# Threshold attention with a two-layer MLP: PV moved to the end of a period, third tile's weights on another engine at the start, last copy split by rows

## The chip, the cores and the metric

The kernel runs on one core of one Trainium2 chip. The metric is the time of one execution on the device in microseconds (us), as the median of several runs; lower is better. The profile of one execution shows five engines, which run side by side and wait for each other through semaphores: TensorE (PE, with its weight loads as PEld), VectorE (DVE), ScalarE (ACT), GpSimd (POOL) and SyncE (SP, which issues most of the DMA transfers).

## The reference

There are 8 batches of 8 heads with 576 tokens of 64 values. Per head, scores are formed, those further than tau below the row's maximum are dropped, the rest go through a softmax, and the result is multiplied by V. The heads of a token, side by side, give a row of 512 values, and two dense layers with a leaky ReLU between them follow.

```python
def _attn_ref(q, k, v, tau):
    scale = 1.0 / np.sqrt(q.shape[-1])
    scores = scale * np.matmul(q, k.transpose(0, 1, 3, 2))
    thresh = np.max(scores, axis=-1, keepdims=True) - tau
    scores = np.where(scores >= thresh, scores, -1000000000.0)
    scores = scores - np.max(scores, axis=-1, keepdims=True)
    attn = np.exp(scores)
    attn = attn / (np.sum(attn, axis=-1, keepdims=True) + 1e-09)
    return np.matmul(attn, v)            # (8, 8, 576, 64)

x = attn_out.transpose(0, 2, 1, 3).reshape(4608, 512)
h = x @ moe_w_in                         # (512, 2048)
out = np.maximum(0.01 * h, h) @ moe_w_out  # (2048, 512)
```

## The kernel before

**Periods.** The attention is cut into 72 periods, n = 0 to 71. A period is one block of 128 query tokens (index m) for four heads (two pairs, index pp), or a "tail": the last 64 tokens of all heads of a batch. Two periods with the same tokens give the 128 x 512 input x of one group of the dense layers, so there are 36 groups. The order of instructions on every engine is the order in which the program issues them; there is no scheduler that reorders. The loop over n issues the work of one period, and the work of three different periods is in it: the scores of period n, the transposing of the weights of period n - 1 (`before`), and the product with V of period n - 2 (`due`, `PV_LAG = 2`).

**What a period does, in TensorE's order.** `scores` (L296) writes four tiles of 128 x 576 scores into five PSUM banks `sc`; each is the sum of three products of half-precision parts. `turn` (L186) transposes q and k of a batch to come, 16 transposes in most periods. `spread` (L401) turns the reciprocal row sums of `due`. Then come two halves. Each has up to two `layer2` steps (L470, 128 x 512 into the bank `o`) and one `layer1` unit (L457, a quarter of a group's hidden layer). The first half also has `pv(due)` (L417, 20 matmuls) behind its layer 1 and, in periods 0 to 2, 5, 7 and 8, four 32-bit transposes `turn32(late)` (L211) ahead of PV.

**VectorE.** `copy_min` (L332) copies each score tile to SBUF with its sign changed and takes the row minimum. `recip` (L376) and the thresholds (L347) follow. Then `evacuate(due)` (L436, L428 for tails) scales the PV product into x, and `weights` (L369) applies the mask to three tiles. In periods with `late`, `take_low` (L239) stands between the first and the second mask.

**ScalarE.** It copies the turned parts of q and k (L249), the spread reciprocals (L407), computes the exponentials `exp_plain` (L358) of the three tiles that VectorE masks, the leaky ReLU of layer 1 (L460), and all of the fourth tile's weights: `exp_steep` does a steep Prelu (L363) and an exponential that sums the row (L364). Every second period it copies a finished output block out of `o` (L478). `take_high` (L232) is its part of the 32-bit transposes.

**Transposed weights.** From period 3 on the weights `w` of a period are transposed by a DMA that SP issues in the following period (`turn_w`, L380). For periods 0 to 2 TensorE does it (`turn_w_here`, L388) and `take_w` (L393) copies the result on ScalarE and VectorE; the steps for tiles 2 and 3 are at the start of the next period. GpSimd splits q and k into two halves (L160, L167, L171); the first such step of a period waits for the last mask of the period before.

**Layer queues.** `evacuate` puts four layer-1 units on the list `l1q` when a group's x is complete. `layer1` takes one, and puts the two layer-2 steps that follow from it on `pending`; `settle` moves `pending` to `l2q`, and is called at the start of every `layer1`. So a layer-2 step runs two halves after its unit.

**Buffers.** The results of `turn`, `turn32`, `spread`, `layer1` and `pv` share two PSUM buffers with the tag "h". In the scores of periods 0 to 2 a no-op on ScalarE (L325), from period 3 on one on GpSimd, signals between two row halves that share a bank.

**The end.** The last group's output is copied by ScalarE (L475, columns 0 to 255) and VectorE (L476, columns 256 to 511), and stored by two DMAs, one on ScalarE's queue and one on SP's (L492).

Of the kernel before, what the change touches and what calls it, by code (L numbers as in the profile page):

```python
# [33 lines left out]
def kernel(  # L34
# [10 lines left out]
    nc = tc.nc  # L45
# [309 lines left out]
    def exp_plain(st, n):  # L355
        t = TILES[n]
        st.e[t] = sb.tile([128, 576], FP16, tag=f"e{n}", bufs=1, name="e")
        nc.scalar.activation(out=st.e[t][:, :], in_=st.s[t][:, :], func=AF.Exp, bias=st.mn[:, n : n + 1], scale=-1.0)  # L358

    def exp_steep(st, n):  # L360
        c, h = t = TILES[n]
        z = st.s[t][:, :]
        nc.scalar.activation(out=z, in_=z, func=AF.Prelu, bias=st.th[:, n : n + 1], scale=-1.0, alpha=1e20)  # L363
        nc.scalar.activation(out=w_of(st, t), in_=z, func=AF.Exp, bias=minus_tau[:, :], scale=1.0,  # L364
                             accum_out=st.sum[:, c, h : h + 1])
# [26 lines left out]
    def take_w(st, first, n, o, copy):  # L392
        return copy(out=st.wt[:, :, :, :].rearrange("k c n q -> k (c n) q")[:, ds(first, n), :],  # L393
                    in_=o.rearrange("k (n q) -> k n q", q=128))
# [14 lines left out]
    def pv(st):  # L409
        st.pv = ps.tile([128, 2, 128], FP32, tag="h", bufs=2, name="pv")  # L410
        n = 64 if st.tail else 128
        for c, u in ((c, u) for c in range(2) for u in range(128 // n)):
            pair = 2 * c + u if st.tail else 2 * st.pp + c
            for i in range(5):
                for h in range(2):
                    blk = i if h == 0 else 9 - i
                    nc.tensor.matmul(out=st.pv[ds(64 * h, 64), c, ts(u, n)], lhsT=v16[st.b % 2][:, pair, blk, :],  # L417
                                     rhs=st.wt[:, c, blk - (blk > 4), ts(u, n)],
                                     start=(i == 0), stop=(i == 4), skip_group_check=True)
# [44 lines left out]
    def layer2():  # L464
        g, r = l2q.pop(0)
        if r == 0:
            g.o = ps.tile([128, 512], FP32, tag="o", bufs=1, name="o")
        for j in (2 * r, 2 * r + 1):
            for c in range(2):
                nc.tensor.matmul(out=g.o[ds(64 * c, 64), :], lhsT=g.g[:, j, ds(64 * c, 64)],  # L470
                                 rhs=w_out16[:, j, :], start=(j == 0), stop=(j == 15), skip_group_check=True)
        if r == 7:
            g.out = sb.tile([128, 512], FP32, tag="osb", bufs=3, name="osb")
            if g.where == (B - 1, 3):
                nc.scalar.activation(out=g.out[:, 0:256], in_=g.o[:, 0:256], func=AF.Copy, bias=0.0, scale=1.0)  # L475
                nc.vector.tensor_copy(out=g.out[:, 256:512], in_=g.o[:, 256:512])  # L476
            else:
                nc.scalar.activation(out=g.out[:, :], in_=g.o[:, :], func=AF.Copy, bias=0.0, scale=1.0)  # L478
            stores.append(g)

    def store():
        g = stores.pop(0)
        b, m = g.where
        if m is None:
            for u in range(2):
                nc.sync.dma_start(out=out[ds((b + u) * S + MAIN, 64), :], in_=g.out[ds(64 * u, 64), :])
        else:
            rows = out[ds(b * S, MAIN), :].rearrange("(p t) f -> p t f", t=4)
            parts = (nc.scalar, nc.sync) if g.where == (B - 1, 3) else (nc.sync,)
            for i, eng in enumerate(parts):  # L490
                f = ts(i, 512 // len(parts))
                eng.dma_start(out=rows[:, m, f], in_=g.out[:, f])  # L492


    loads_at, turns_at, early32, late32, split_at_, pool_at = {}, {}, {}, {}, {}, {}
# [120 lines left out]
    while n < N + PV_LAG or l1q or pending or l2q or stores:  # L616
        st = periods[n] if n < N else None
        before = periods[n - 1] if 1 <= n <= N else None
        due = periods[n - PV_LAG] if PV_LAG <= n < N + PV_LAG else None
        here = before and before.n < 3  # L620
        keys, now32, late = turns_at.get(n, []), early32.get(n, []), late32.get(n)


        if st:
            scores(st)
        bank = turn(keys) if keys else None
        for x in now32:
            turn32(x)
        if here:
            before.wt = sb.tile([128, 2, 9, 128], FP16, tag="wT", bufs=4, name="wT")  # L630
            bank = ps.tile([128, 1024], FP16, tag="h", bufs=2, name="tp")
        if due:
            bank = spread(due, bank)
        if here:
            turn_w_here(before, 12, 6, bank[:, 0:768])
        for key in keys:
            take(key, 0, on_act)
        if due:
            take_spread(due, bank)
        for x in now32:  # L640
            take_high(x)
        if here:
            take_w(before, 12, 6, bank[:, 0:768], on_act)
        if st:
            copies(st, before, lambda: [take(key, 1, on_dve) for key in keys], now32)
            exp_plain(st, 0)
        elif before:
            recip(before)
        work = [lambda key=key: split_pool(key) for key in split_at_.get(n, [])] + pool_at.get(n, [])
        for i, f in enumerate(work):  # L650
            mm = f()
            if i == 0 and before:
                behind_masks(mm, before)
        for key in keys:
            if key[1:] == ("t", "k"):
                widen_keys(key[0])
        if n < 4:
            idle((16, 10, 8, 4)[n], spare("o"))
        if here:
            o = ps.tile([128, 1024], FP16, tag="o", bufs=1, name="wp")  # L660
            if n < 3:
                turn_w_here(before, 0, 8, o)
        elif before and st:
            turn_w(before)
        landed = [f() for f in loads_at.get(n, [])]
        while stores:
            store()
        if n == 0:

            for i in range(4):  # L670
                tc.add_manual_dep(load_w(i).ins, w_behind.ins.name, BEHIND, reason="DMA would serve w_in first")


        if due and (n == 3 or n > N):
            pv(due)
            if n > N:
                evacuate(due)
        if n == 3:
            turn_w_here(before, 0, 8, o)
            idle(12, spare("h"))  # L680
        for half in range(2):
            if half == 1 and n == 3:
                exp_steep(st, 3)
            for _ in range(2):
                if l2q:
                    layer2()
            if l1q:
                layer1()
            elif n >= N:
                settle()  # L690
            if half == 0:
                if st:
                    exp_plain(st, 1)
                    exp_plain(st, 2)
                if here:
                    take_w(before, 0, 8, o, on_act)
                if late:
                    turn32(late)
                    take_high(late)
                if n == N:  # L700

                    before.wt = sb.tile([128, 2, 9, 128], FP16, tag="wT", bufs=4, name="wT")
                    free = [(sc[:, ts(i, 512)].bitcast(FP16), 8 * i, m) for i, m in enumerate((8, 8, 2))]
                    for o, first, m in free:
                        turn_w_here(before, first, m, o)
                if due and n <= N:
                    if n != 3:
                        pv(due)
                    evacuate(due)
                if n == N:  # L710
                    a, *more = [take_w(before, first, m, o[:, 0 : 128 * m], on_dve if first else on_act)
                                for o, first, m in free]
                    for x in more:
                        tc.declare_no_dep(x.ins, a.ins, reason="other banks")
            elif st and n != 3:
                exp_steep(st, 3)
        if here:
            o = ps.tile([128, 512], FP16, tag="o", bufs=1, name="wp")
            turn_w_here(before, 8, 4, o)
        for i in range(3 if st else 0):  # L720
            weights(st, i)
            if late and i == 0:
                take_low(late)
            if here and i == 1:
                take_w(before, 8, 4, o, on_dve)
        n += 1
# [1 line left out]
_INS = ['q', 'k', 'v', 'tau', 'moe_w_in', 'moe_w_out']  # L728
# [31 lines left out]
```

## Time and profile before

| | |
|---|---|
| median of 3 runs | 483.85 us (482.97 to 485.55) |
| the profiled execution | 484.76 us; its span, from the first to the last instruction, is 482.9 us |
| granted TensorE clock | 1.00 in all of the span |
| busy: PE, DVE, ACT, POOL | 465.4, 434.8, 418.4, 190.9 us |
| chain that ended last | PE 75%, DMA 13% (12% of it the transposed weights), ACT 6% |
| one mask (L369), one score copy (L332) | 0.816 us, 0.753 us |
| one plain exponential (L358) | 0.778 us |
| steep pair (L363, L364) | 0.767 and 0.775 us, and 0.187 us for reading the sum |
| x from PV (L436) | 0.424 us |

"Busy" is the time in which an engine works on an instruction; the share of the span is that over 482.9 us. The times of one instruction are means of start to end, and successive instructions of an engine overlap a little, so that a mask takes 0.74 us from start to start. The chain is followed back from the last instruction, at each step to what released it. The starts of the score products mark the periods in the trace: period 5 begins at 43.13 us, period 9 at 71.69, period 71 at 455.95.

### The profile page before, as it was taken

How to read it: one execution, taken by the hardware profiler on the slowest of the kernel's cores; microseconds unless marked ns; L12 is line 12 of the kernel's file. 1: busy time of each engine (PE TensorE's matmuls, PEld its weight loads, DVE VectorE, ACT ScalarE, POOL GpSimd, SP SyncE). 2: the span in 40 equal slices, each digit the busy share in tenths (PEclk: the TensorE clock that was granted, in tenths of full speed). 3: DMA queues.
4: the chain of work that ended last, by engine and by line, in shares of the span. 5: the costliest groups of instructions: out<-in, count | busy, mean ns of one | idle time of the engine just before them, and what ended most of it. 6: DMA issues, size and time to landing. Idle time of an engine off the chain costs nothing.

```text
span 482.9 us, 25246 instructions
## 1 busy us (share of the span) xinstructions
PE 465.4 (96%) x10858; PEld 378.9 (78%) x10858; DVE 434.8 (90%) x1315; ACT 418.4 (87%) x777; POOL 190.9 (40%) x313
## 2 busy tenths in 40 slices
PE   7779999999999999999999999999999999999996
PEld 5567788888887788888887788888878888777785
DVE  4999989999999999999999999999998999999940
ACT  3888889999998899998998999999998899988862
POOL 2544436543554444353454554353454444000000
PEclk9999999999999999999999999999999999999999
DMA  9999998898979989799989969898989988657851
GB/s 177 237 210 218 193 224 167 160 192 194 190 165 207 182 165 188 151 177 192 193 167 215 209 142 189 150 194 181 203 167 184 215 168 135 124 122 123 122 96 45
DMA packets 216480, 83.68 MB, mean 173 GB/s; under 512 B 186032, under 2 KB 211888, under 8 KB 216368
## 3 DMA queue, kind: packets, MB, share of 16 engines
q1 hardware_dynamic: 210672, 77.42, 83.2%
q0 software_dynamic: 4224, 4.19, 5.3%
q8 instruction: 85, 1.39, 1.2%
q10 hardware_dynamic: 1472, 0.46, 0.4%
q14 instruction: 27, 0.22, 0.1%
HBM read 36.70 MB, written 9.44 MB: 96 GB/s over the span
## 4 chain that ended last, share of the span: by engine, by line
PE 75%; DMA 13%; ACT 6%; DVE 2%; issue 2%; SPq 0%; POOL 0%; ACTq 0%; POOLq 0%; DVEq 0%
PE hp L457 22%; PE o L470 22%; PE sc L296 18%; DMA wT<-w 12%; PE pv L417 8%; PE tp L401 3%; PE tp L186 2%; ACT e L358 1%; DVE w L369 1%; ACT w L364 1%; DMA vrawt<-in_v_dram 1%; ACT s L363 1%; ACT wT L393 1%; DMA raw<-in_k_dram 1%; DVE s L332 1%
## 5 line engine op out<-in xcount | busy, mean ns | idle before, releaser
L332 DVE TENSOR_SCALAR_CACHE_REDUCE s<-sc 128x576 f32<-128x576 f32 x288 | 205.4, 753 | 15.9 <-PE sc L296 15.8
L457 PEld LDWEIGHTS <-win 128*64 128x64 f16 x4608 | 146.8, 110 | 29.1 <-issue 1.4
L369 DVE SCALAR_TENSOR_TENSOR w<-s,th,e 128x576 f16<-128x576 f32 x216 | 166.3, 816 | 0.2
L358 ACT ACTIVATE e<-s,mn 128x576 f16<-128x576 f32 x216 | 159.7, 778 | 0.0
L470 PE MATMUL o<-wout,g 128*64 128x512 f16 x1152 | 149.3, 379 | 0.5 <-issue 0.5
L457 PE MATMUL hp<-x,win 128*64 128x128 f16 x4096 | 136.7, 219 | 0.3 <-DVE kT L249 0.3
L460 ACT ACTIVATE g<-hp 128x512 f16<-128x512 f32 x144 | 86.2, 598 | 44.5 <-PE hp L457 44.5
L296 PE MATMUL sc<-kT,qT 64*128 64x384 f16 (+7 forms) x1920 | 119.6, 284 | 0.7 <-DVE kT L239 0.7
L296 PEld LDWEIGHTS <-qT 64*128 64x128 f16 (+1 forms) x1920 | 90.3, 97 | 16.4 <-issue 1.4
L160 POOL TENSOR_SCALAR scaled<-raw 128x512 f32<-128x512 f32 x53 | 32.8, 620 | 169.0 <-DVE w L369 158.5
L470 PEld LDWEIGHTS <-g 128*64 128x64 f16 x1152 | 58.9, 110 | 28.6 <-ACT g L460 0.3
L171 POOL TENSOR_TENSOR half<-scaled,half 128x512 f16<-128x512 f32 (+1 forms) x68 | 71.8, 1056 | 5.8
L417 PE MATMUL pv<-wT,v 128*64 128x128 f16 (+1 forms) x1600 | 53.3, 215 | 4.9 <-DMA wT<-w 3.7
L364 ACT ACTIVATE w<-s,minus_tau 128x576 f16<-128x576 f32 x72 | 55.8, 775 | 2.3
L363 ACT ACTIVATE s<-s,th 128x576 f32<-128x576 f32 x72 | 55.2, 767 | 0.0
L417 PEld LDWEIGHTS <-v 128*64 128x64 f16 x1600 | 45.8, 110 | 6.6 <-PE hp L457 4.5
L167 POOL CAST half<-scaled 128x512 f16<-128x512 f32 (+1 forms) x68 | 38.4, 564 | 4.4
L436 DVE TENSOR_TENSOR x<-pv,by 128x256 f16<-128x256 f32 x64 | 27.1, 424 | 9.4 <-PE pv L417 5.7
L407 ACT COPY by<-tp 128x256 f16<-128x256 f16 x72 | 26.8, 372 | 3.4 <-PE tp L388 3.4
L186 PEld LDWEIGHTS <-half 64*128 64x128 f16 x968 | 24.4, 95 | 2.4 <-issue 1.5
L186 PE MATMUL tp<-ident,half 64*128 64x64 f16 x968 | 24.4, 190 | 0.0
L113 POOL CAST v<-vraw 128x256 f16<-128x256 f32 x64 | 24.1, 410 | 0.0
(58 smaller groups left out, 311.9 us busy)
## 6 DMA issues: line engine op xcount, KB each, us to landing
vraw<-in_v_dram SPq DMA_DIRECT2D x16, 512.0 KB, 5.2
out_dram<-osb SPq DMA_DIRECT2D x31, 256.0 KB, 5.0
raw<-in_q_dram SPq DMA_DIRECT2D x13, 512.0 KB, 5.6
raw<-in_k_dram SPq DMA_DIRECT2D x13, 512.0 KB, 4.9
win<-in_moe_w_in_dram POOLq DMA_DIRECT2D x4, 512.0 KB, 11.2
wout<-in_moe_w_out_dram POOLq DMA_DIRECT2D x4, 512.0 KB, 14.9
raw<-in_q_dram SPq DMA_DIRECT2D x12, 128.0 KB, 3.9
raw<-in_k_dram SPq DMA_DIRECT2D x10, 128.0 KB, 4.2
```

The source lines that it names most:

```text
L171: nc.gpsimd.tensor_tensor(out=halves[key][:, 1, 0:n, :, :], in0=scaled.pop(key)[:, 0:n, :, :], in1=halves[key][:, 0, 0:n, :, :], op=AX.sub ...
L186: nc.tensor.transpose(tps[key][r][:, x, t, :], half[rows, x, t, :, :].rearrange("p h d -> p (h d)"), ident[rows, rows])
L296: yield nc.tensor.matmul(out=o, lhsT=lhs, rhs=turned[st.b, "k"][rows, kx, pair, ds(key0, n)], start=(i == 0), stop=(i == 2), skip_group_ch ...
L332: return nc.vector.tensor_scalar(out=st.s[TILES[n]][:, :], in0=sc[:, ds(PLACE[TILES[n]], 576)], scalar1=-1.0 / UNIT, scalar2=None, op0=AX. ...
L358: nc.scalar.activation(out=st.e[t][:, :], in_=st.s[t][:, :], func=AF.Exp, bias=st.mn[:, n : n + 1], scale=-1.0)
L363: nc.scalar.activation(out=z, in_=z, func=AF.Prelu, bias=st.th[:, n : n + 1], scale=-1.0, alpha=1e20)
L364: nc.scalar.activation(out=w_of(st, t), in_=z, func=AF.Exp, bias=minus_tau[:, :], scale=1.0, accum_out=st.sum[:, c, h : h + 1])
L369: st.last = nc.vector.scalar_tensor_tensor(out=w_of(st, t), in0=st.s[t][:, :], scalar=st.th[:, n : n + 1], in1=st.e[t][:, :], op0=AX.is_le ...
L417: nc.tensor.matmul(out=st.pv[ds(64 * h, 64), c, ts(u, n)], lhsT=v16[st.b % 2][:, pair, blk, :], rhs=st.wt[:, c, blk - (blk > 4), ts(u, n)] ...
L457: nc.tensor.matmul(out=hp[ds(64 * c, 64), jj, :], lhsT=w_in16[:, i, ds(128 * (4 * u + jj) + 64 * c, 64)], rhs=g.x[:, i, :], start=(i == 0) ...
L460: nc.scalar.activation(out=g.g[:, ds(4 * u, 4), :], in_=hp[:, :, :], func=AF.Prelu, bias=0.0, scale=1.0, alpha=0.01)
L470: nc.tensor.matmul(out=g.o[ds(64 * c, 64), :], lhsT=g.g[:, j, ds(64 * c, 64)], rhs=w_out16[:, j, :], start=(j == 0), stop=(j == 15), skip_ ...
```

## The change

From period 5 to period 71 `pv(due)` is issued behind both halves, as TensorE's last product of a period, and `evacuate(due)` behind the three masks. Periods 2 to 4 and 72 on keep their order. A half without a layer-1 unit now calls `settle` in every period, not only from period 72 on. In periods 1 and 2 the third tile's weights are computed by `exp_steep` on ScalarE, in the second half, instead of by `exp_plain` and a mask on VectorE. The last output block is copied by rows instead of columns: ScalarE takes rows 0 to 63, VectorE rows 64 to 127, declared independent of each other, and the two stores are split the same way.

```diff
@@ layer2
             if g.where == (B - 1, 3):
-                nc.scalar.activation(out=g.out[:, 0:256], in_=g.o[:, 0:256], func=AF.Copy, bias=0.0, scale=1.0)
-                nc.vector.tensor_copy(out=g.out[:, 256:512], in_=g.o[:, 256:512])
+                a = nc.scalar.activation(out=g.out[0:64, :], in_=g.o[0:64, :], func=AF.Copy, bias=0.0, scale=1.0)
+                x = nc.vector.tensor_copy(out=g.out[64:128, :], in_=g.o[64:128, :])
+                tc.declare_no_dep(x.ins, a.ins, reason="other rows")
@@ store
             for i, eng in enumerate(parts):
-                f = ts(i, 512 // len(parts))
-                eng.dma_start(out=rows[:, m, f], in_=g.out[:, f])
+                n = 128 // len(parts)
+                eng.dma_start(out=rows[ts(i, n), m, :], in_=g.out[ts(i, n), :])
@@ the loop over n
+        late_pv, plain = 5 <= n < N, 2 if 1 <= n < 3 else 3
...
             if l1q:
                 layer1()
-            elif n >= N:
+            else:
                 settle()
             if half == 0:
                 if st:
-                    exp_plain(st, 1)
-                    exp_plain(st, 2)
+                    for i in range(1, plain):
+                        exp_plain(st, i)
...
-                if due and n <= N:
+                if due and (n < 5 or n == N):
                     if n != 3:
                         pv(due)
                     evacuate(due)
...
             elif st and n != 3:
-                exp_steep(st, 3)
+                for i in range(plain, 4):
+                    exp_steep(st, i)
         if here:
             o = ps.tile([128, 512], FP16, tag="o", bufs=1, name="wp")
             turn_w_here(before, 8, 4, o)
-        for i in range(3 if st else 0):
+        if late_pv:
+            pv(due)
+        for i in range(plain if st else 0):
             weights(st, i)
             if late and i == 0:
                 take_low(late)
             if here and i == 1:
                 take_w(before, 8, 4, o, on_dve)
+        if late_pv:
+            evacuate(due)
         n += 1
```

## The prediction

> **What bounds the kernel now.** I read the page first, then every period's busy times (the windows view, one stretch from each start of the score products to the next), then the waits, then the timeline of the periods that stand out.
>
> ```profile
> PE 465.4 (96%) x10858; PEld 378.9 (78%) x10858; DVE 434.8 (90%) x1315; ACT 418.4 (87%) x777; POOL 190.9 (40%) x313
> ```
>
> TensorE leads, with VectorE close behind. Per period (columns: length, then busy time of PE, PEld, DVE, ACT, POOL, clock, DMA share, GB/s):
>
> ```profile
> 50.39:57.55 7.16, 6.46 (x158) 5.23 (x154) 7.15 (x21) 6.24 (x12) 3.65 (x6) 1.00 1.09 200
> 64.54:71.69 7.15, 6.89 (x152) 5.81 (x150) 6.57 (x20) 6.33 (x12) 2.92 (x6) 1.00 1.02 260
> 133.54:139.65 6.11, 6.11 (x147) 5.02 (x144) 5.94 (x19) 5.47 (x10) 3.08 (x5) 1.00 0.79 146
> 145.77:152.59 6.82, 6.30 (x148) 5.18 (x145) 6.05 (x19) 5.47 (x10) 2.86 (x7) 1.00 1.02 219
> 258.19:265.31 7.12, 6.31 (x148) 5.19 (x146) 6.06 (x19) 5.47 (x10) 2.85 (x7) 1.00 0.99 216
> ```
>
> These are periods 6, 8, 19, 21 and 39. A plain period is 6.11 us and TensorE is busy in all of it: it is the bound, and an order that only moves its work gains nothing there. Periods 21 and 39 are longer, and TensorE is idle in them. The timeline of period 21 says where:
>
> ```profile
> 148.57 1.06 PE L457 MATMUL hp<-x,win 128*64 128x128 f16 x32
> 150.16 0.75 PE L417 MATMUL pv<-wT,v 128*64 128x128 f16 x20 [0.52 <-DMA wT<-w]
> 150.71 1.06 PE L470 MATMUL o<-wout,g 128*64 128x512 f16 x8
> ```
>
> PV starts 1.59 us after layer 1, elsewhere 0.89: 0.70 us lost to the transposed weights, which come by DMA.
>
> ```profile
> PE pv L417 <- DMA wT<-w: 3.7, 7, 0.8
> DVE s L332 <- PE sc L296: 15.8, 62, 0.4
> DVE osb L476 <- ACT osb L475: 10.4, 1, 10.4
> DMA to landing us min/median/max: 4.5/6.2/9.4
> ```
>
> The second row is VectorE's slack (some 0.23 us in a period); the last is the weights' transpose (L380). In periods 5 to 8 no engine is full, since they wait for each other:
>
> ```profile
> 68.33 0.66 PE L211 MATMUL tp<-ident,raw 128*128 128x128 f32 x4
> 69.25 0.75 PE L417 MATMUL pv<-wT,v 128*64 128x128 f16 x20 [0.26 <-ACT g L460]
> ```
>
> **PV behind both layer steps, periods 9 to 71.** Nothing is added: the 20 matmuls (0.56 us from start to start) go from between the two halves to the end. The 0.10 us that layer 1 takes longer ahead of the scores (0.99 against 0.89) should then follow PV. In period 19's times PV starts 3.70 us after the scores, later 5.45: the DMA gets 1.75 us more. The delays of PV, as its start after layer 1 less 0.89, are 0.70, 0.71, 0.42, 0.98, 0.66 and 0.38 us (periods 21, 23, 33, 39, 41, 58), all below 1.75, so all go: **-3.8**. A stall removed lets the next transpose meet busier queues (21 with 23: 1.4; 39 with 41: 1.6), still below 1.75. Bounds: 0 to -4.8, the latter with what those periods lose besides.
>
> On VectorE x (0.42 busy, 0.34 to the next start) changes places with three masks (0.74 each): the masks end 0.34 earlier, and x where they ended, 0.23 us before the copy that waits for the scores. PV ends about 0.7 us before x begins. POOL's splits, which wait for the last mask, start 0.34 earlier; POOL is 40% busy, so 0. On ScalarE the second leaky ReLU is ready 0.56 earlier and ends up to 0.39 sooner, and with it the steep weights, behind which SP's transpose waits. Every other period the output copy (0.59) moves from the first half to the second, since the layers run half a period later; the steep weights are then 0.07 later, covered by ScalarE's 0.22 us wait for layer 1. Sum 0.
>
> **Periods 5 to 8.** Half a layer step leaves: period 5 has no second layer-1 unit (0.99), period 6 no second layer-2 step (0.86); the added `settle` keeps the remaining steps in line. But TensorE isn't the bound here. Following VectorE, its first copy of the scores starts in period 6 at 51.92 (before: 51.97). The 0.80 us wait of x for PV goes, but the low half of the late transposes (L239) now reaches VectorE early and waits some 0.76 us for ScalarE's high half (L232). Period 7: 58.47 (58.91); period 8: 66.07 (66.11).
>
> TensorE meets a new wait in periods 7 and 8. There the late transposes (L211) hold one of the two PSUM buffers "h" until a vector operation issued behind PV frees it; the other holds the second layer-1 result. So PV waits for the ReLU just before it. Period 7: layer 1 ends at 63.19, ScalarE has the high half until 63.3, the ReLU takes 0.60 from 63.4, PV starts at 64.05 (0.86 lost), scores of period 8 at 64.71 (64.54). Period 8: layer 1 ends at 70.85, ScalarE does the two exponentials, the high half and the output copy (now here) until 71.45, then the ReLU; PV at 72.1 (1.25 lost), scores of period 9 at 72.75 against 71.69: **+1.0**. Behind the waiting PV stand the scores, for which VectorE waits. Bounds: -0.5 (VectorE's chain alone) to +1.5; I take the TensorE chain, since its order is fixed.
>
> **Third tile on ScalarE in periods 1 and 2.** VectorE loses a mask (0.74) each, ScalarE gets a steep pair (21.39 to 23.07: 1.68) for a plain exponential (0.67). TensorE turns the weights when both are done; now the mask's end sets that (24.28, TensorE at 24.34). ScalarE would end at 18.00 + 2 x 0.67 + 0.89 (copy) + 0.49 (high half) + 2 x 1.68 = 24.08, and TensorE start at about 24.2. The no-op of L325 is queued on ScalarE behind the added pair, so period 2's scores finish at about 23.75 instead of 22.98; with the transposes behind them that is 24.25, no later. Period 2 the same way: 26.0 + 6.08 and 0.1 for the release, 32.2 against 32.24. The bound passes from VectorE to ScalarE at the same height: **-0.04**, bounds -0.7 (a mask) and +0.5 (the no-op, a further third of the pair).
>
> **The end.** The half step that left period 5 comes back: one more layer-1 unit and layer-2 step behind the last score products, 0.89 + 0.87 = 1.76, all TensorE time that nothing hides. Period 72's first layer 1 needs the x of period 71, now behind the masks (462.9; layer 1 was at 462.71): +0.24. **+2.0**.
>
> The last copies each get 64 rows of 512. ScalarE: 0.59 (its 128x512 row). VectorE: 0.69 (between 0.425 for 128x256 f32 and 0.68 for 128x1024 f16; the 128x512 f32 of L239 took 0.69). VectorE's copy started after ScalarE's (479.51 against 479.09), so the last store left at 479.96. Side by side it leaves at about 479.83: **-0.13**; one behind the other, +0.45. No row shows two engines on one PSUM bank at once. The declared independence lets them start together, and I take that. The Trainium skill, "PSUM — Partial Sum Buffer", section "PSUM bank collisions raise a hardware error", says that two engines may use one bank at the same time in different quadrants of 32 partitions, but not in the same ones; by that rule the halves by rows run side by side, as in the sum, while the halves by columns could not have.
>
> **Sum.** -3.8 + 1.0 - 0.04 + 2.0 - 0.13 = -1.0 us. The profiled execution took 484.76 (span 482.9 and 1.86 around it), so it would take 483.8. It is 0.9 above the median of 483.85, about what period 55 lost (6.99 us for 6.11) in gaps that the waits view gives to "issue" and not to any engine. I count those as chance and predict 483.0.
>
> **Rivals.**
> *A, the sum: 483.0, chance 0.52.*
> *B, the two-buffer wait is hidden.* If VectorE's chain sets periods 7 and 8, +1.0 becomes 0, and with up to 0.7 from the early masks it is 481.2. For: VectorE is busy for 7.15 of 7.16 us in period 6. Against: PV stands in line ahead of the scores. 0.20.
> *C, the transposes stay late.* The DMA share is near 1.0 in the stalled periods; if PV waits half as long in its new place, 1.9 us come back: 484.9. Against: each measured delay is below the 1.75 gained. 0.12.
> *D, slower: the next transposes wait for x.* PV's buffer is now freed by x at the end of VectorE's chain, and the next period's transposes (L186, L401) write there. They start 0.12 us after the copy for which VectorE has 0.23 to spare; x's tail (0.08) and the release (0.06) leave about 0.2. If VectorE ends later than that, each 0.1 us costs 6.2 over 62 periods: 489.2. For: VectorE is 94 to 98% busy. Against: its work is unchanged. 0.11.
> *E, the copies are not parallel:* 0.45 instead of -0.13: 483.6. 0.05.
>
> The gains and losses nearly cancel. A measurement here can tell about 0.5%, 2.4 us, from no change (481.4 to 486.3). Faster needs B at its better end: 0.20. Slower is D and a little of A and C: 0.14. Same: 0.66. The range runs from B with half a microsecond more to C with the early and the period-8 terms at their bad ends, 480.4 to 486.0; D is left out.
>
> **What would show it.** Right: the row "PE pv <- DMA wT" nearly gone, periods 21 to 58 at 6.11 or less, period 9's scores near 72.7, "PE pv <- ACT g" up by 2 us, some 2 us more behind the last scores, and the two final copies starting together. Wrong: periods 9 to 63 longer than 6.15 with transposes waiting for x (D), new waits for wT (C), or TensorE's first scores of period 9 before 71.7 (B).

## The result and the profile after

The changed kernel took 486.84 us (median of 10 runs, 485.15 to 490.01) beside 484.06 for the kernel before (10 runs): a ratio of 1.006, 95% interval 1.0034 to 1.0086, so slower by 0.6%. The forecast was 483.0 and "the same", with a range of 480.4 to 486.0. The profiled execution took 488.6 us with a span of 486.8; the granted clock was 1.00. Measured once more on another occasion the ratio was 1.0019 (0.999 to 1.0049). Two executions of one kernel differ by 2 us and more, so below every step is placed by the length of its stage in several traces.

The page's first line of after, which answers to the first line shown of before: nearly the same work, with four instructions moved from VectorE to ScalarE.

```profile
PE 466.9 (96%) x10858; PEld 378.4 (78%) x10858; DVE 439.4 (90%) x1311; ACT 420.2 (86%) x781; POOL 190.4 (39%) x313
```

The windows view of after, one stretch for each of the periods 6, 8, 19, 21 and 22 (columns: length, then busy time of PE, PEld, DVE, ACT, POOL, clock, DMA share, GB/s):

```profile
50.62:57.72 7.10, 5.56 (x150) 4.71 (x146) 6.73 (x21) 4.94 (x12) 3.64 (x6) 1.00 1.12 187
65.49:73.27 7.78, 7.02 (x153) 5.55 (x150) 6.67 (x21) 6.17 (x12) 2.92 (x6) 1.00 1.05 262
135.16:141.28 6.12, 6.12 (x149) 5.03 (x146) 6.03 (x19) 5.87 (x12) 3.08 (x5) 1.00 0.54 103
147.39:154.09 6.70, 6.35 (x148) 5.30 (x144) 6.40 (x21) 5.86 (x12) 2.85 (x7) 1.00 1.29 200
154.09:161.07 6.98, 6.24 (x139) 5.18 (x137) 5.93 (x19) 5.27 (x11) 2.95 (x4) 1.00 1.28 250
```

A plain period is still 6.1 us. Period 8 is 7.78 instead of 7.15, and period 21 still loses 0.6 us, although PV no longer waits there. Period 22 takes 6.98 us; in before it lost nothing:

```profile
152.59:158.59 6.00, 6.00 (x139) 4.90 (x138) 5.69 (x19) 5.64 (x11) 2.96 (x4) 1.00 0.93 195
```

The waits of TensorE in after:

```profile
PE pv L417 <- DMA wT<-w: 1.7, 1, 1.7
...
PE pv L417 <- DVE qT L239: 1.5, 2, 0.8
PE hp L457 <- issue: 1.4, 3, 0.7
...
PE tp L186 <- issue: 0.4, 1, 0.4
```

The first row is one wait, in period 5. From period 9 on PV's waits for the transposed weights are gone, as forecast, but for one of 0.25 us in period 59. In their place stand gaps that the profile puts down to "issue": TensorE waits for no engine and no transfer. The timeline of after in periods 21 and 22 shows where they lie:

```profile
150.20 0.61 PE L457 MATMUL hp<-x,win 128*64 128x128 f16 x15
151.16 0.69 PE L457 MATMUL hp<-x,win 128*64 128x128 f16 x17 [0.35 <-issue]
...
156.78 0.39 PE L457 MATMUL hp<-x,win 128*64 128x128 f16 x7
157.91 0.91 PE L457 MATMUL hp<-x,win 128*64 128x128 f16 x25 [0.74 <-issue]
```

One run of 32 matmuls of layer 1, with the same operands and one PSUM buffer throughout, breaks off after the 15th and another after the 7th. No buffer and no semaphore lies between those instructions, so the cause has to be sought in the instructions themselves. They come by DMA too; the table of the DMA queues has a row for them (packets, MB, share of 16 engines):

```profile
q8 instruction: 85, 1.39, 1.2%
```

85 packets of 16 KB. TensorE has 21,716 matmuls and weight loads, 255.5 for each packet, so I take it that a packet carries 256. I numbered TensorE's instructions in the trace in order (matmuls, weight loads and semaphore waits) and set the gaps of periods 9 to 71 beside the packets (times in us; k counts the packets from 0, the instructions count from 1; "since" is the start of the last instruction before the gap):

```
packet k   lands    TensorE stops at         since    resumes   behind the landing
22         149.59   instr. 256*22 + 449      150.59   151.16    1.57
23         156.44   256*23 + 449             156.95   157.91    1.47
31         198.48   256*31 + 449             199.50   200.08    1.59
39         240.61   256*39 + 449             241.59   241.99    1.38
43         263.23   256*43 + 449             264.04   264.60    1.38
45         274.91   256*45 + 449             275.91   276.18    1.26
```

Every gap stands at the same place of a block of 256, and TensorE goes on 1.3 to 1.6 us after packet k has landed. So the theory (1) is: TensorE runs out of instructions. (The expectations below give the same place as 434, counted without the 14 semaphore waits ahead of it and from 0.) The packets travel on the 16 DMA engines that also carry loads and transposes. In the quiet stage behind 430 us of after a packet begins no later than 0.7 us past the point 269 instructions ahead of the stop; in periods 21 and 22 it begins 3.9 and 5.1 us past it. The rival is that the gaps belong to the new order: its buffers, or certain of its instructions.

### The profile page after: what moved, and what is told of

The parts are those of the page before. It is cut to its first block, busy times and chain, and to the rows that moved or that the text cites. A ratio compares the mean times of both kernels' runs of the same rounds, so it can differ in the third digit from the quotient of the medians.

```text
span 486.8 us, 25121 instructions
## 1 busy us (share of the span) xinstructions
PE 466.9 (96%) x10858; PEld 378.4 (78%) x10858; DVE 439.4 (90%) x1311; ACT 420.2 (86%) x781; POOL 190.4 (39%) x313
## 4 chain that ended last, share of the span: by engine, by line
PE 84%; ACT 6%; DVE 3%; DMA 3%; issue 1%; SPq 0%; DVEq 0%; ACTq 0%
PE hp L457 24%; PE o L470 24%; PE sc L296 21%; PE pv L417 8%; PE tp L401 3%; PE tp L186 3%; ACT e L358 2%; DMA wT<-w 2%; DVE w L369 1%; DVE s L332 1%; ACT wT L393 1%; DMA raw<-in_k_dram 1%; ACT g L460 1%; ACT s L363 1%; ACT w L364 1%
## 5 line engine op out<-in xcount | busy, mean ns | idle before, releaser
L358 ACT ACTIVATE e<-s,mn 128x576 f16<-128x576 f32 x214 | 157.9, 773 | 0.0
L460 ACT ACTIVATE g<-hp 128x512 f16<-128x512 f32 x144 | 85.5, 594 | 27.9 <-PE hp L457 27.9
L364 ACT ACTIVATE w<-s,minus_tau 128x576 f16<-128x576 f32 x74 | 57.4, 776 | 2.4
L417 PE MATMUL pv<-wT,v 128*64 128x128 f16 (+1 forms) x1600 | 53.7, 215 | 5.7 <-ACT e L358 1.8
L363 ACT ACTIVATE s<-s,th 128x576 f32<-128x576 f32 x74 | 57.3, 775 | 0.0
L417 PEld LDWEIGHTS <-v 128*64 128x64 f16 x1600 | 46.0, 110 | 7.4 <-DMA wT<-w 4.4
L249 ACT COPY kT<-tp 128x512 f16<-128x512 f16 x27 | 15.8, 584 | 11.2 <-PE tp L401 11.1
```

Source lines behind the costliest of these rows:

```text
L460: nc.scalar.activation(out=g.g[:, ds(4 * u, 4), :], in_=hp[:, :, :], func=AF.Prelu, bias=0.0, scale=1.0, alpha=0.01)
```

## Experiments

For each kernel the stages as read from its trace (us: scores of period 5 begin; periods 5 to 8; periods 9 to 71; from period 71's scores to the end; span), then, within periods 9 to 71, the waits that the profile puts down to the transposed weights, and number and sum of pauses at instruction 256k + 449 (over 0.25 us from the start of one instruction to the start of the next). Each row is one execution:

```
                       p5     5-8    9-71    end    span    wT    stops
before                43.13  28.56  384.27  26.94  482.9   2.6   1  0.9
e_early               43.07  30.10  384.28  26.94  484.4   2.9   0
e_copy                43.42  28.82  383.32  27.49  483.0   0.6   1  0.3
copy_rows_store_cols  43.28  28.85  384.41  27.39  483.9   3.0   0
spread_before         43.44  29.07  383.41  26.94  482.9   1.0   0
spread_early          42.82  29.19  387.43  26.94  486.4   5.4   0
even_early            42.83  29.54  388.43  26.95  487.7   5.2   2  1.7
before_shift          43.42  30.00  385.27  26.95  485.6   1.8   4  3.0
light_before          44.49  28.59  379.14  27.11  479.3   0     0
after                 42.67  30.60  383.87  29.68  486.8   0     6  3.3
after_again           43.68  29.54  384.51  29.69  487.4   0.3   8  3.9
e_pv                  44.21  29.36  385.67  29.12  488.4   0     8  5.7
e_pv9                 43.37  29.28  382.65  29.12  484.4   0     5  2.8
spread_after          42.94  29.38  382.87  29.69  484.9   0     6  3.2
even_after            42.81  29.64  385.36  29.68  487.5   0     9  6.0
after_shift           42.82  30.38  381.00  29.75  483.9   0     2  1.3
late9_shift           42.55  30.68  380.25  29.11  482.6   0     1  0.6
light_after           42.97  29.36  380.05  30.08  482.5   0     1  0.6
light_after_shift     42.95  30.28  379.50  30.26  483.0   0     0
```

In a few of the old order's rows further waits of PV for the same transposes are put down to ScalarE (1.4 and 0.7 in e_copy), so "wT" is a lower bound there.

### The parts of the change, one by one

```diff
+        late_pv = 5 <= n < N
...
-            elif n >= N:
+            else:
                 settle()
...
-                if due and n <= N:
+                if due and n <= N and not late_pv:
...
+        if late_pv:
+            pv(due)
...
+        if late_pv:
+            evacuate(due)
```

This is e_pv; e_pv9 has `9 <= n < N`.

> The move of PV and x (with the settle) alone; early periods and last copies as before. Theory 1 (the stall is traded: the waits for the transposed weights go, and TensorE's own instruction fetch, which lies on the same busy DMA engines, comes late instead; the rest of the loss is the half step, given back at the end, and waits in periods 5 to 8): nearly the whole loss of the change, 486.7 us (484.06 before, +2.0 in periods 5 to 8, -0.4 to -1.4 in periods 9 to 71, +2.1 at the end). PV's wait for the transposes nearly zero, and some 2 to 3 us of gaps put down to issue. Theory 2 (the order is sound, and the row-wise stores or the third tile's weights cost it): 484.0 or less. The prediction's sum for this part alone, -3.8 + 1.0 + 2.0, says 483.3.

Measured: 487.24, ratio 1.0017 (0.9999 to 1.0035). The time alone is between the two theories. The trace is not: no wait for the transposes is left, eight stops cost 5.7 us, and the end is 2.18 us longer than before.

> The third tile's weights on ScalarE in periods 1 and 2 alone. By the prediction's step -0.04, so 484.0; by the two traces period 5 starts 0.46 us earlier, so 483.6. A rival has a gain in those periods eaten up by period 8, since transposes of later periods come by loads that keep their times: 484.0 with period 9 at 71.7.

(`plain = 2 if 1 <= n < 3 else 3`, with the loops over `exp_plain`, `exp_steep` and `weights` as in the change.) Measured: 486.67, ratio 1.0019 (0.9996 to 1.0043), which tells it from neither. In the trace period 1 takes 7.18 us (7.85 before) and period 3 8.16 (7.63), in every kernel that has this part. From the first scores to period 5 it is 34.7 to 34.9 us with it and 34.8 to 35.1 without it, in the median 0.2 less. In the two traces that is gains against a loss, none of which the prediction had: 0.67 in period 1 (of the mask's 0.74) and 0.25 in period 2, of which period 3 gives 0.53 back.

> The last copy and its two stores by rows, alone. By the prediction's step -0.13: 483.9. By the two traces +0.5: 484.6, with 4.35 us instead of 3.81 from the start of the first last copy to the end, of which the copies win 0.2 and the stores of 64 rows of 2 KB lose 0.7 (2.5 and 2.7 us to landing instead of 1.9 and 2.0).

(The last hunk of the change alone.) Measured: 487.42, ratio 1.0023 (0.9999 to 1.0047). The end grows from 26.94 to 27.49. The timeline of e_copy:

```profile
478.70 0.69 DVE L476 COPY osb<-o 64x512 f32<-64x512 f32 x1 [10.03 <-PE o L470]
478.70 0.59 ACT L475 ACTIVATE osb<-o 64x512 f32<-64x512 f32 x1 [1.15 <-PE o L470]
479.32 0.55 ACTq L493 DMA_DIRECT2D out_dram<-osb  x1
479.42 0.47 SPq L493 DMA_DIRECT2D out_dram<-osb  x1
```

The copies do run side by side. But ScalarE's copy takes 0.59 us instead of the 0.38 of 128 rows of 256, so the first store leaves 0.62 us after the copies' start instead of 0.42. The second leaves at 0.72 instead of 0.87. They land after 2.5 and 2.7 us, before after 1.9 and 2.0.

> PV behind both layer steps and x behind the masks from period 9 on instead of 5; nothing else of the change. Theory 1: the two-buffer waits of periods 7 and 8 and the late transposes of 5 and 6 stay out; the half step leaves periods 9 and 10, where TensorE is the bound and 1.76 us are won, and comes back at the end (+2.1); the stalls are traded as before (-0.4 to -1.4): 483.4 to 484.4, so no loss, about 2.7 less than the PV move from period 5. Theory 2 (the order itself costs in every period, wherever it begins): 486 or more.

Measured: 487.23, ratio 1.0039 (1.0011 to 1.0068): this expectation was wrong, and in an instructive place. Periods 9, 10 and 11 take 5.34, 6.49 and 6.70 us, together 18.53 against 18.75 before. Of the half step of 1.76 us that is taken out there, 0.22 is won. The timeline of e_pv9:

```profile
79.60 0.20 PE L186 MATMUL tp<-ident,half 64*128 64x64 f16 x1
80.59 0.39 PE L186 MATMUL tp<-ident,half 64*128 64x64 f16 x15 [0.79 <-DVE x L436]
...
86.09 0.20 PE L186 MATMUL tp<-ident,half 64*128 64x64 f16 x1
86.56 0.39 PE L186 MATMUL tp<-ident,half 64*128 64x64 f16 x15 [0.27 <-DVE x L436]
```

TensorE, now ahead, meets VectorE's chain: the transposes need the buffer that x frees behind the masks (the place of rival D). The two waits shown are 1.06 of the 1.54 us that are missing. VectorE is only a few tenths behind TensorE, so TensorE gains little by work taken away at this spot. The half step comes back at the end at its full price.

### The same two orders with less DMA traffic

```diff
+            if b < 2:
                 at(loads_at, rows[i], lambda b=b, s=s, w_=w_: load_main(b, s, w_))
...
+            if b < 2:
                 at(loads_at, v_at[s], lambda b=b, s=s: load_v(b, s))
```

(The readers of these buffers take batch 1's, so the two kernels leave out the loads of six batches, and their output is not the reference's.)

> The kernel before, without the loads of q, k and v (main tokens) for batches 2 to 7: POOL converts batch 1's buffers again, so the output is not the reference's; every other instruction stays. Theory 1 (the busy DMA queues make the transposes late, and in other places TensorE's instruction fetch): PV's waits for the transposes vanish from period 9 on, periods 21, 39 and 41 fall to 6.11, and the time is 0.7 to 1.0% below before. Theory 2 (the transposes are late because SP issues them late): the same, since SP issues fewer loads; the landing times tell: by theory 1 the transposes land after 4 to 5 us instead of 6.2 in the median.

> The kernel after with the same loads left out. Theory 1: its issue gaps in periods 9 to 71 vanish too (fetches of 256 TensorE instructions land well before TensorE comes to the place where it stops), so the stage takes the same time as in the lighter kernel before, within 0.3 us apart from periods 13, 31 and 49 (0.24 each), and the two differ by periods 5 to 8 (0.8 to 2.0) and the end (2.7) less the early 0.4: 3 to 4.5 us. Rival (the gaps come from the new order itself, its buffers or its instructions): 2 to 3 us of gaps stay in periods 9 to 71, and it is 5 to 7 us behind the lighter kernel before.

Measured: light_before 480.8, ratio to before 0.9909 (0.988 to 0.9939); light_after 484.34, 0.9979 (0.9962 to 0.9996). The traffic falls from 83.7 to 64.8 MB, the transposes land after 5.8 us instead of 6.2 in the median and after 7.6 instead of 9.4 at worst. Waits and stops both vanish but for one. The long stage takes 379.14 and 380.05 us, 5.1 and 3.8 less than in before and after. So both losses come from the same traffic. Without them the new order wins nothing: it is 0.9 behind, with 0.56 for the one stop and some 0.2 each in periods 13, 31 and 49 for a later start of TensorE's transposes, less 0.15 in period 9.

By the expectation the weights' transposes should have landed after 4 to 5 us in light_before, and 5.8 in the median misses that. Its theory 2 (they are issued late) is refuted all the same by the two traces: the six transposes for which PV waited in before in periods 21, 23, 33, 39, 41 and 58 were issued 2.3 to 2.4 us after the start of their period, as in light_before, and landed after 7.5 to 8.3 us instead of 4.6 to 6.4. The stop that stays, in the timeline of light_after, period 29:

```profile
196.93 0.23 PE L187 MATMUL tp<-ident,half 64*128 64x64 f16 x3
197.53 0.37 PE L187 MATMUL tp<-ident,half 64*128 64x64 f16 x13 [0.37 <-issue]
```

After breaks off after the same third transpose of that period; the rival had this for it.

### Other times for the loads

```diff
-            rows, t_at, v_at = (E - 3, E - 2, E + 2, E + 3), (E + 1, E + 6), (E + 1, E + 4, E + 2)
+            rows, t_at, v_at = (E - 3, E - 2, E, E + 3), (E + 1, E + 6), (E + 1, E + 4, E + 2)
```

> The kernel before with one 512 KB load of each odd batch (the second k) issued two periods earlier, so that four loads in a row become three with a free period between; all else the same. Theory 1: the waits of periods 21 and 23, 39 and 41 fall (they were 0.7, 0.7, 1.0 and 0.7), 1 to 2.5 us less: 0.3 to 0.5% below before. If the waits only move to other periods, within 0.1%.

> The kernel after with the same load earlier. Theory 1: its issue gaps of periods 21, 22, 39, 41 and 42 shrink, 1 to 2 us, and it stays 2 to 4 us above the kernel before with the spread loads, which is the end and periods 5 to 8. Rival (gaps of the order itself): unchanged against after, 0.2 to 0.6% above before.

Measured: spread_before 0.9986 (0.997 to 1.0003), spread_after 1.0026 (1.0005 to 1.0048). The stalls only moved: spread_before loses nothing in period 41, but period 21 takes 7.66 us (6.82 before), and spread_after has as many stops as after.

The even batches' loads evened out as well (`even_early`, `even_after`: rows E - 12, E - 11, E - 8, E - 6 and v at E - 9 and E - 5):

> The kernel before with the loads of q, k and v for batches 2 to 7 put into two of three periods in turn (at most two 512 KB loads in a row where five stood in six periods), and the third tile's weights on ScalarE. If the waits come from bursts of the DMA, those of periods 9 to 71 fall from some 4 us to 0 to 1.5, and with 0.4 from the early periods it is 0.6 to 0.9% below before: the version that beats both. If the queues are simply full, the waits move to other periods: within 0.2% of before.

> The kernel after with the same evened loads. Theory 1: the issue gaps fall like the waits of the other kernel, and what is left against it is the end (2.7), periods 5 to 8 (0.8) and the waits of periods 13, 31 and 49 (0.7): 4 us, so about before's time, 0.0 to 0.3% below it. Rival (gaps of the order): no better than after.

Measured: even_early 1.0143 (1.009 to 1.0195), even_after 1.0027 (0.9998 to 1.0056). My schedule was a bad one: period 45 of even_early takes 9.33 us, most of it one wait of 3.0 for a transpose. That the waits come from bursts which a hand can smooth is not shown. The old order met it with long waits of PV, the new one with nine stops. spread_early, the last try of this kind:

> The kernel before with the one load of each odd batch two periods earlier (which alone gave 0.14% less) and the third tile's weights on ScalarE (0.38 us less by period 5 in five traces): if both hold, 1.0 us or 0.2% below before; it would be the fastest of the real versions, though less than this measurement tells from no change. If one of the two is chance, equal to before.

Measured: 1.001 (0.9989 to 1.003); in its trace one wait of PV in period 39 lasts 3.3 us, and in the 2.7 us behind it the granted clock was 0.57. It is no faster version.

### A second trace of after, and the last stores

> The kernel after, unchanged, timed beside the others and traced a second time. Theory 1 says that its parts against before are fixed at the end (+2.7), in periods 0 to 4 (-0.4) and in periods 7 and 8 (+1.4), while the stage of periods 9 to 71 and period 5 vary from one execution to the next with the DMA traffic: 2 to 4 us above before, with issue gaps in other periods than in the first trace, each at the same place in TensorE's instructions (434 past a multiple of 256). Rival (the gaps belong to particular instructions of the new order): the same gaps in the same periods.

Measured: 487.3, 1.0019 (0.999 to 1.0049), so 0.9 us above before in place of the 2 to 4 expected. Eight stops, all at 449. Periods 21, 22 and 42 are free of them now, 15, 36 and 57 have one; but 29, 35, 39 and 41 have theirs again. That fits both theories, since the places at 449 are the same in both traces, and so it decided nothing. Periods 5 and 6 together took 13.55 us here and 15.04 in the first trace: that stage varies by over 1 us from one execution to the next.

> The kernel before with the last copy split by rows, side by side, and its two stores still by columns (each behind both copies). If the shape of the stores is the cost (64 rows of 2 KB land 0.6 to 0.7 us later than 128 rows of 1 KB), then the stores land after 1.9 to 2.0 us again and from the first copy's start to the end it takes 3.6 to 3.7 us (before 3.81, by rows throughout 4.35). If starting both stores at once is the cost, it stays above 4.1.

(Only the copies' half of the last hunk; one execution.) From the copies' start to the end it took 4.25 us, against 3.81 in before and 4.35 in e_copy, so this expectation failed. The table of DMA issues for its last 4 us (KB each, us from issue to landing):

```profile
out_dram<-osb SPq DMA_DIRECT2D x1, 128.0 KB, 2.3
out_dram<-osb ACTq DMA_DIRECT2D x1, 128.0 KB, 2.4
```

Stores of the old shape that leave together land after 2.3 and 2.4 us; half a microsecond apart it was 1.9 and 2.0; together and in rows of 2 KB, 2.5 and 2.7. By one trace of each, leaving at once is most of the cost, the shape the smaller part. The Trainium skill, "DMA: Bandwidth & Descriptors", section "Rules for kernel authors", advises against two transfers of disjoint partition halves, since both spread over the same 16 engines and share them. The 2.5 and 2.7 us fit that, but halves by columns that left together (2.3 and 2.4) were slowed too.

### Moving the instruction stream against the work

The fillers of periods 0 to 2, at half their width and twice their number: 136 more TensorE instructions (68 products and their weight loads) ahead of period 3, and nothing else.

```diff
-            idle((16, 10, 8, 4)[n], spare("o"))
+            idle((32, 20, 16, 4)[n], spare("o"), 256 if n == 3 else 128)
```

> The lighter kernel after (batch 1's q, k, v converted again for batches 2 to 7, so the output is not the reference's) with the filler products of periods 0 to 2 at half their width and twice their number: 136 more TensorE instructions ahead of everything else, no other change. Its one gap (0.56 us in period 29, before a transpose of q or k) was at instruction 434 past a multiple of 256. Theory 1 (TensorE stops where its fetched instructions end): period 29 falls to 6.24 us, because the place where it could stop has moved by 136 instructions; a gap in another period, if there is one, is again 434 past a multiple of 256. Rival (the gap belongs to those transposes, or to what they wait for): period 29 stays at 6.8 us, at the same transpose.

> The kernel after with the same 136 added filler instructions. Theory 1: all its issue gaps change periods (in two traces of after periods 29, 35, 39, 41 and 59 had one each time), each again at 434 past a multiple of 256; the time stays within 0.4% of after, 0.1 to 0.7% above before, since the DMA is as busy as it was. Rival: periods 29, 35, 39, 41 and 59 keep their gaps.

Measured: in light_after_shift (one execution) no stop is left; period 29 takes 6.24 us. after_shift took 485.47, ratio to before 0.9979 (0.9962 to 0.9997), lower than the 0.1 to 0.7% above before that were expected. It has two stops, in periods 32 and 45, where there had been none; 29, 35, 39 and 41 have lost theirs. (The gap of period 59 in the expectation was a wait for transposed weights, not a stop.) The timeline of after_shift in period 29 has the same 16 transposes in one piece:

```profile
197.94 0.41 PE L186 MATMUL tp<-ident,half 64*128 64x64 f16 x16
```

and the windows view gives that period as

```profile
196.34:202.58 6.24, 6.24 (x172) 5.02 (x168) 6.02 (x19) 5.97 (x12) 2.39 (x3) 1.00 0.78 105
```

against this line of after:

```profile
197.87:204.69 6.82, 6.43 (x172) 5.10 (x169) 6.14 (x19) 5.96 (x12) 2.39 (x3) 1.00 0.65 104
```

The work is the same, only the cut of the instruction stream has moved. This decides against the rival. A control and the sum of the good parts:

> The kernel before with the same 136 added filler instructions, as a control. Theory 1: its losses in periods 9 to 71 are waits of PV for the transposed weights, which do not depend on where the instruction stream is cut; they stay at 3 to 5 us in periods 21, 23, 33, 39, 41 and the like, and the time is within 0.15% of before. Rival (the fillers themselves help, by a better start or otherwise): 0.3% or more below before.

> Behind both layer steps from period 9 on instead of 5, the third tile's weights on ScalarE, last copy and stores by columns as before, and the 136 filler instructions. From the parts measured, against before: early -0.4, periods 5 to 8 as before, periods 9 to 11 -0.2, periods 11 to 71 at 368 to 369 instead of 371 to 372 (-3), the end +2.2: -1.4 us, 0.3% below before, and some 0.7 us below the kernel after with the fillers (0.55 of it the stores). If the cut of the instruction stream falls badly here, gaps of 0.3 to 1 us come back at 434 past a multiple of 256 and it is level with before.

Measured: before_shift 1.0002 (0.997 to 1.0034), so the fillers alone are no gain. But its trace has four stops (3.0 us), which the expectation did not foresee: the old order can run out of instructions as well. Nor did PV's waits stay where they were: periods 21, 23 and 58 lose nothing now, and "wT" fell to 1.8. Counted with its semaphore waits the stops lie at 449 too, and so does the gap of period 55 in the first trace of before. Over all 19 traces, in periods 9 to 71, there are 54 such pauses, and TensorE resumed 1.26 to 1.65 us after the landing in each. The other way round it holds as well: TensorE passed that place 1,359 times, and never sooner than 1.23 us after the landing of its packet. Of the 64 other pauses over 0.25 us, 60 are waits for a buffer or for data, and four lie in the low clock of spread_early.

late9_shift took 484.34, ratio 0.9963 (0.9936 to 0.999): faster than before, by its interval at least 0.1%. After was not timed beside it, but came out above before both times. Its long stage is 380.25 us, 4.0 below before, and 2.2 of that goes back at the end.

## Why the prediction was wrong

**The step that failed: "all below 1.75, so all go: -3.8".** The waits did go. But the term took for granted that TensorE would then be limited by its work alone. It was limited by the arrival of its instructions on the same busy DMA: in the traces of after, after_again and e_pv the stops take 3.3 to 5.7 us. In the two shown traces the stage of periods 9 to 71 became 383.87 from 384.27 (-0.4). Over the traces with the given loads and fillers the medians are 384.5 (after, after_again, e_pv) and 384.3 (before, e_early, e_copy, copy_rows_store_cols). So the term was +0.2, not -3.8. Rival C (the transposes stay late) had the right suspicion of the DMA, but the wrong victim. That the gain exists in principle is shown by after_shift, with 381.0: there 3.3 of the 3.8 were got, by a cut that happened to fall well.

Why the packets come too late so often in after is open. It is not that PV's waits had given them time. In before seven such waits fell in the last 269 instructions ahead of the place; taking each wait off the time by which the packet was early (an estimate), the packets would still have landed 1.65 us ahead of TensorE in one case and 2.3 or more in the others. What differs is that more packets begin late: over 2.8 us past the mark of 269 instructions 5 of 72 in before, 11 of 71 in after. The new order also has 56 instructions fewer, the waits at PV, so its stream is cut elsewhere, and with the fillers the old order has more stops than the new (4 and 2, one trace each). How much belongs to the order and how much to the cut is not shown.

**"I count those as chance", of period 55's 0.9 us.** It was the one sign of the mechanism in the profile of before: the same stop, at the same place of a block. A gap put down to "issue" in the middle of equal instructions was a resource that I did not name.

**Periods 5 to 8, +1.0: the two buffers were right, the one waited for was not.** PV did lose time in periods 7 and 8. But the prediction let it wait for the ReLU, and it waited for the other buffer, the late transposes', which the low half (L239) frees. In after's timeline:

```profile
64.81 0.75 PE L417 MATMUL pv<-wT,v 128*64 128x128 f16 x20 [0.77 <-DVE qT L239]
...
71.84 0.69 DVE L239 SCALAR_TENSOR_TENSOR qT<-tp,qT 128x512 f16<-128x512 f32 x1 [0.36 <-ACT qT L232]
72.18 0.61 ACT L460 ACTIVATE g<-hp 128x512 f16<-128x512 f32 x1
...
72.58 0.75 PE L417 MATMUL pv<-wT,v 128*64 128x128 f16 x20 [0.76 <-DVE qT L239]
```

In period 8 PV starts 0.05 us after L239 ends and 0.21 before the ReLU (L460) does. So the row "PE pv <- ACT g" did not grow by 2 us; "PE pv <- DVE qT L239" appeared. TensorE stood idle for 0.77 and 0.76 us, against 0.86 and 1.25 forecast. Period 9 began at 73.27 (forecast 72.75): layer 1 of period 7 already came some 0.7 us later than forecast, since in periods 5 and 6 PV also waited 1.65 and 1.54 us for transposes. (The profile puts the second wait down to ScalarE; the transpose landed 0.04 us before PV's start.)

Over six traces with the late PV from period 5 the stage has a median of 29.6 us, over the ten others with all loads 29.2: +0.4, within the bounds, with groups that overlap (29.4 to 30.6 and 28.6 to 30.7). That the size fits is luck in part. By the same medians periods 7 and 8 take 1.9 us more and periods 5 and 6, which lose half a layer step, 1.4 less; the forecast had both smaller. Of the +2.04 between the two first traces 1.42 lie in periods 7 and 8. Rival B is refuted: periods 7 and 8 take 7.8 to 8.3 us wherever PV is late.

**Third tile on ScalarE, -0.04:** -0.2, inside its bounds, but as the sum of gains in periods 1 and 2 and a loss in period 3 that were not foreseen.

**The end, +2.0:** e_pv alone +2.18. Right. In periods 5 and 6 the half step is in part won back, and the waits of periods 7 and 8 take more than that; e_pv9 won 0.22 of it, since there VectorE, not TensorE, had the last word.

**The last copies, -0.13: +0.55.** The copies ran side by side, and rival E is out. The mis-sized term was what follows them: I took the moment the last store leaves for the end, and did not cost the landing of two stores that leave together, nor the first one leaving later. The Trainium skill, "PSUM — Partial Sum Buffer", section "PSUM bank collisions raise a hardware error", allows two engines on one bank in different quadrants; the two copies starting at 478.70 agree.

**Rival D** cost little where it was placed: some 0.2 us each in periods 13, 31 and 49, 0.6 in all instead of 6.2.

With the measured terms the sum is -0.2 + 0.4 + 0.2 + 2.2 + 0.55 = 3.15 us; the medians differ by 2.8, and by 0.9 in the second measurement. The price of the change was there from the start (the half step and the stores), and its gain went into another wait.

## What to carry to other kernels

A wait for a late DMA is not won by moving its consumer alone: ask what else comes by the same busy engines, the instructions included, and test it with less traffic rather than with more slack. A gap "issue" inside a run of equal instructions is a clue: number the instructions, and if they share a place in blocks of 256, as here, compare them with the landing of the instruction packets. Work moved out of a stage counts only if its engine sets the pace there; where two engines run a few tenths apart, price it with the second engine's slack.

## What the runs showed of the hardware that was not expected

- TensorE's instructions arrive during the run, 256 in a packet of 16 KB, on the DMA engines of the data. In the quiet stage a packet took 0.9 to 1.5 us from start to landing; under load it began up to 5.2 us past the mark (e_pv), and TensorE stopped for up to 1.5 us (e_pv, even_after).
- It stopped for want of them at one place only, at instruction 449 past a multiple of 256, and resumed 1.26 to 1.65 us after the landing (54 pauses). Semaphore waits count as instructions: before has 56 of them at PV (L417), after none.
- 136 filler instructions at the start of a program moved later stops enough to change the long stage by 3 us (383.9 and 384.5 in the two traces of after, 381.0 in the one of after_shift), without any change in the other work. Only one such shift was tried on each order; which cut is best, and whether it would stay so with other loads, is open.
- Two 128 KB stores of the same shape that leave together took 0.3 to 0.5 us longer to land than two that leave 0.45 apart (2.3 and 2.4 us in copy_rows_store_cols, 2.0 and 1.9 in before).
